# Moving the k^T v and o copies of one attention pair from VectorE and a later place to ScalarE, directly behind a copy out of PSUM

## The chip, the cores and the metric

The kernel runs on one core of a Trainium2 chip. The metric is the device time of one execution in microseconds; lower is better. Within a core several engines run side by side, each through a queue of its own in program order: TensorE (PE in the profile; PEld is its weight load), VectorE (DVE), ScalarE (ACT), GpSimd (POOL) and SyncE (SP), which here issues nearly all DMA transfers. They meet only at semaphores. Matmul results land in PSUM, in banks that have to be read by ScalarE or VectorE before TensorE may write them again.

## The reference

An attention without softmax is normalised and goes through a wide layer with an unusual gate:

```python
kv = einsum('bhsd,bhse->bhde', k, v)          # (8, 8, 64, 64)
o = einsum('bhsd,bhde->bhse', q, kv)          # (8, 8, 576, 64)
x = o / sqrt(mean(o * o, -1) + 1e-6) * g_norm # to (4608, 512)
h = x @ w_in                                  # w_in (512, 2048)
g = h * erf(log(1 + exp(h)))
out = g @ w_out                               # w_out (2048, 512)
```

Inputs q, k, v are fp32 of shape (8, 8, 576, 64); the weights arrive as float64.

## The kernel before, in words

**Groups.** The 4608 tokens are worked on in nine groups of 512: the first 512 tokens of each of the eight batch elements, and a ninth group of the last 64 tokens of all of them, which are collected in `x_last` on the way. Heads are taken in pairs, four pairs to a group. T counts the groups (0 to 8), p the pairs.

**The wide layer.** Groups 0 and 1 go through 16 steps each, n = 0 to 31 (L1188); step f of a group makes 128 of the 2048 hidden columns. In group 1 (T = 1, n = 16 to 31) a step multiplies numbers that were split into a high, a low and a combined part: `hidden` (L855) and `product` (L802) put eight matmuls into the PSUM tile `n_ps` and four into `m_ps`. The two tiles come in turn out of the two banks of `ps_h`, so step n + 1 writes `n_ps` once step n's was read, and `m_ps` likewise. ScalarE copies `n_ps` out, scaled (L1248, "the copy of n"), VectorE adds `m_ps` to it (`add`, L788), ScalarE takes the softplus of the sum (L1262), later the erf (L1186), and VectorE multiplies the two (`gates`, L1114). The last eight hidden tiles of group 1 aren't multiplied with w_out by the plain path: 28 to 31 are taken over by the main loop, and 24 to 27 (`whole - BATCH` to `whole - 1`) are split into `g_held` (`hold_upper` on ScalarE, L748; `hold_lower` on VectorE, L751 and L754) and are multiplied after the loop in `held_sums` (L1142; its matmuls are L1130). `held_sums` first multiplies units 24 and 25 into `o_ps` (they need the combined part, L754) and into two `n_ps`, then unit 26, then unit 27; ScalarE copies the `n_ps` out (`scaled`, L1161). Behind it the main loop over groups 2 to 8 begins (L1355), which fetches the split weights back from DRAM (`load_parts`, L1059, `w_in_parts` and `w_out_parts`); the first four w_out loads can be issued only when the memory of the loop's tiles is free.

**Attention of the next group, inside the steps.** While group 1 goes through its 16 steps, the pairs of group 2, the third group, are prepared: `attention(2, p)` (L454) returns pieces, and `pieces_of` (L1063) lays them into the lists of the steps. `steps[f][3]` and `steps[f][0]` run at the beginning of step f, `steps[f][1]` behind its softplus. For pair p they begin at f = 4p: `visit` (in `steps[4p + 1][1]`) multiplies q with the pair's k^T v, and k with v for the next pair, into a PSUM tile `at_ps` of two banks, and lets ScalarE square o (L492). Then ScalarE copies o out (`copy_out`, L507), the off-diagonal halves of k^T v (`kv_beside`, L368) and the last tokens (L517); `keep` on VectorE adds the halves (`kv_sum`, L372) into `bd_kv`; `sums` on VectorE transposes the squares (L539), sums them in blocks (L415) and brings blocks together (L428, L429). `mean`, `norm` and `split` turn them into the normalised x in three parts.

**The fourth pair of the third group** (T = 2, p = 3, f = 12) is different: `both` is true. From the next group on, pairs are taken two at a time, so it makes k^T v for two pairs. Its `visit` is in step 13 and its `keep` and `sums` at the beginning of step 14 (n = 30). Here the four copies of k^T v halves and the copy of the last tokens are made by VectorE inside `keep`, followed by two sums; and `copy_out` is put into `steps[14][1]`, behind step 14's softplus. Its `mean`, `norm` and `split` are run by `held_sums`.

**Order.** Each engine runs its instructions in the order in which the Python code issues them. So at step 14 VectorE has, one after the other: the gates of step 13, the four copies, `x_last`, the two sums, L539, L415, L428 and L429, step 14's addition (L788), one gate (L1114), and the lower parts of units 24 and 25; at step 15 the addition (L788) and the lower parts of 26 and 27. ScalarE has in step 14: the copy of n, the softplus, the copy of o, the upper parts of units 26 and 27; then step 15's copy of n and softplus, a table load and the roots (L433 to L435), another table load (L1163), and `scaled`.

Of the kernel before, what the change touches and what calls it, by code (L numbers as in the profile page):

```python
# [70 lines left out]
def kernel(  # L71
# [10 lines left out]
    nc = tc.nc  # L82
# [8 lines left out]
    FC = DF // P  # L91
# [242 lines left out]
    def halves_of(t):  # L334
        return t.rearrange("p (a t) -> p a t", a=2)

    def kv_of(T, p):
        return bd_kv[:, (T * NP + p) % 2, :]
# [52 lines left out]
    def other_tile(n):  # L391
        t = attp.tile([P, 2, 2, D], FP32, name="kv_other", tag="kv_other")
        return t[:, 0:n]

    def at_tile():
        return at_pool(1).tile([P, 2, G], FP32, name="at_ps", tag="at")
# [57 lines left out]
    def attention(T, p):  # L454

        st = {}

        alone = p > 1
        then = divmod(T * NP + p + 1, NP)
        both = (T, p) == (FIRST, NP - 1)  # L460
        more_cols = slice(kv_cols.stop, kv_cols.stop + D)

        two = halves_of

        bd = kv_of(T, p)

        def visit():


            qT = ready.pop((T, p))  # L470
            at = st["at"] = at_tile()
            x = halves_of(qT[:, 0:G])
            for s in rows_of:
                nc.tensor.matmul(
                    at[s, 1, 2 * P : 2 * P + R], lhsT=bd[s, D : 2 * D], rhs=qT[s, G:S], start=True, stop=True
                )
            st["o"] = at[:, :, 0 : 2 * P]
            for _, product_ in kv_products(*then, at[:, 1, kv_cols], at[:, 0, kv_cols], first=1):
                product_()
            if both:  # L480
                for _, product_ in kv_products(then[0], 1, at[:, 1, more_cols], at[:, 0, more_cols]):
                    product_()
            for a, i in ((0, 0), (0, 1), (1, 0), (1, 1)):
                nc.tensor.matmul(
                    at[rows_of[i if a else 1 - i], a, 0 : 2 * P],
                    lhsT=bd[rows_of[i], a * D : (a + 1) * D],
                    rhs=x[rows_of[i], a],
                    start=True,
                    stop=True,
                )  # L490
            st["sq"] = qT[:, 0:G]
            nc.scalar.activation(two(st["sq"]), st["o"], AF.Square, scale=0.125)  # L492
            if not both:
                copy_out()
                beside(nc.scalar.copy)

        def copy_out():
            if T < FIRST:
                if T not in xT:
                    xT[T] = wide.tile([P, KC, G], FP32, name="xT", tag="ab"[T])  # L500
                x = xT[T][:, p, :]
            elif p % 2:
                x = x_new.tile([P, G], FP32, name="x", tag="x")
            else:
                x = attp.tile([P, G], FP32, name="x_even", tag="sq_lo")
            st["x"] = x
            nc.scalar.copy(two(x), st["o"])  # L507

        def beside(copy):


            others = st["others"] = other_tile(2)
            at = st["at"]
            kv_beside(at, others[:, 0], copy)
            if both:
                kv_beside(at, others[:, 1], copy, more_cols)
            copy(x_last[:, p, T * R : T * R + R], at[:, 1, 2 * P : 2 * P + R])  # L517

        def keep():
            if both:  # L520
                beside(nc.vector.tensor_copy)
            others = st.pop("others")
            kv_sum(*then, st["at"], others[:, 0])
            if both:
                kv_sum(then[0], 1, st["at"], others[:, 1], more_cols)

        def sums():


            if not alone:  # L530
                if p == 0:
                    shared["ms"] = small_tile("ms")
                total = shared["ms"]
            else:
                total = small_tile("ms")
            st["ms"] = total
            side = p if not alone else 0
            t = attp.tile([P, G], FP32, name="sq_t", tag="rms_r")
            nc.vector.transpose(out=t, in_=st["sq"])  # L539
            sum_blocks(total, side, t)  # L540
            shared[side] = st
            if not alone and p == 0:
                return
            n = side + 1
            other = small_tile("ms_other")
            meet(total, other, nc.vector.tensor_copy, n)
            st["n"] = n

        def root(table=True):
            if "n" not in st:  # L550
                return
            total, n = st["ms"], st["n"]
            st["r"], st["u"] = small_tile("rms"), small_tile("rms_u")
            exp_ln_table()
            roots(total, st["r"], st["u"], n)
            if table:
                softplus_table()

        def norm():
            if "n" not in st:  # L560
                return
            n = st["n"]
            refine(st["ms"], st["r"], st["u"], n)
            for i in range(n):
                other = shared[i]
                rb, x = other.pop("sq"), other["x"]
                spread_over(rb, st["u"], i)
                nc.vector.scalar_tensor_tensor(
                    out=x, in0=x, scalar=gm_col, in1=rb, op0=ALU.mult, op1=ALU.mult
                )  # L570

        def split():
            if T < FIRST or "n" not in st:
                return
            for q_ in range(p + 1 - st["n"], p + 1):
                upper(shared[q_ % 2 if not alone else 0]["x"], x_forms[T][0][:, q_])
            for q_ in range(p + 1 - st["n"], p + 1):
                lower(shared[q_ % 2 if not alone else 0].pop("x"), *(form[:, q_] for form in x_forms[T]))

        def loads():  # L580
            i = T * NP + p + 2
            if i == (FIRST + 1) * NP + 1:
                load_q(i)
                load_kv(i + 1)
                load_kv(i + 2)
                return
            load_pair(i, later=True)
            if i == (FIRST + 1) * NP:
                load_kv(i + 1)

        first_ = (partial(prepare, T, p),) if (T, p) == (1, 0) else ()
        then_ = partial(turn, *then)
        pieces = (first_, (visit, loads), (keep, sums))
        later = copy_out if both else chain
        return (*(partial(chain, *group) for group in pieces), later, root, partial(chain, norm, then_), split)


# [189 lines left out]
    def add(out_, ps):  # L787
        nc.vector.tensor_tensor(out=out_, in0=ps, in1=out_, op=ALU.add)  # L788
# [274 lines left out]
    def pieces_of(T):  # L1063


        steps = [([], [], [], []) for _ in range(FC)]
        for p in range(NP):
            products, apply, after, later, mean, norm, split = attention(T, p)
            f = (BATCH - 1) * (p + 1) if T < FIRST else BATCH * p

            first = T < FIRST and p == 0
            steps[f][1].append(products)
            steps[f + 2 if first else f + 1][3 if first else 1].append(apply)
            steps[f + 3 if first else f + 2][3].append(after)
            steps[f + 2][1].append(later)
            with_erf = (f + 2) % BATCH == BATCH - 1
            if T == FIRST and p == NP - 1:
                ending.extend((partial(mean, table=False), norm, split))
                continue
            steps[f + 2][1].append(partial(mean, table=not with_erf))  # L1080
            steps[f + 3][0].append(norm)
            steps[min(f + 4, FC - 1)][0].append(split)
        return steps
# [104 lines left out]
    for n in range(FIRST * FC + 1):  # L1188
        T, f = divmod(n, FC)
        if T < FIRST:  # L1190
            if f == 0:
                steps = pieces_of(T + 1)
# [47 lines left out]
        if T < FIRST:  # L1240
# [4 lines left out]
            if n in plain:  # L1245
                nc.scalar.copy(h, plain.pop(n))
            else:
                nc.scalar.activation(h, n_ps, AF.Copy, scale=SHIFT - 1.0)  # L1248
                add(h, m_ps)
            if T == FIRST - 1:  # L1250
                if n <= whole + 2:
                    gates(done + max(0, n - whole - 1))
                for key in list(w_new):
                    w_lower(*key)
                for key in to_cut[f]:
                    w_upper(*key)
                if n == whole + 1:
                    gates(whole - 2)
# [225 lines left out]
```

## Time and profile before

| | |
|---|---|
| median of 3 runs | 885.76 us (883.95 to 885.78) |
| profiled execution, its time | 885.19 us |
| its span | 883.4 us |
| PE busy | 873.4 us (99%) |
| DVE busy | 751.2 us (85%) |
| ACT busy | 550.7 us (62%) |
| DMA | 259.88 MB, 293 GB/s to and from HBM over the span |

The span is what the trace covers; the time of the profiled execution is 1.8 us longer. All places in time are us from the span's start, so the steps around the change lie at 209 to 224 us. In a row of the timeline the first number is the start, the second the length; in brackets stands how long the engine had been idle before it, and who released it. A row of the waits has the sum, the times and the longest. "x4" is a row of four instructions merged into one.

### The profile page before, as it was taken

To read this page: it belongs to the slowest core of one execution; us is meant where nothing else is said; L and a number is where in the kernel's file an instruction comes from. 1 tells how busy PE (TensorE), PEld (TensorE's weight loads), DVE (VectorE), ACT (ScalarE), POOL (GpSimd) and SP (SyncE) were. 2 spreads that over 40 slices of the span, in tenths; PEclk is the share of its full clock that TensorE was granted. 3 is DMA by queue.
4 is the path that set the end of the run, shared out by engine and by line. 5 is a ranking of instruction groups with operands and counts; after the bars stand their busy time and mean duration, and the time that the engine had idled before them with its cause. 6 is when DMAs were issued, how large, how long until landed. Compare 5 with 4: busy or idle time off the path is not lost.

```text
span 883.4 us, 13264 instructions
## 1 busy us (share of the span) xinstructions
PE 873.4 (99%) x4842; PEld 653.1 (74%) x4842; DVE 751.2 (85%) x1122; ACT 550.7 (62%) x808; POOL 4.7 (1%) x14
## 2 busy tenths in 40 slices
PE   8999999999999999999999999999999999999998
PEld 4444455565778888888888888888888888888887
DVE  5889987899889898989898989898979797966667
ACT  5967675686675657565665647474757575755552
POOL 2000000000000000000000000000000000000000
PEclk9999999999999999999999999999999999999999
DMA  9976428889699987998799979998887779778861
GB/s 288 292 253 183 147 75 326 311 314 355 229 341 411 341 346 246 395 326 347 232 379 350 351 236 349 374 328 297 281 344 281 293 267 359 294 275 334 314 257 48
DMA packets 136928, 259.88 MB, mean 294 GB/s; under 512 B 78816, under 2 KB 87264, under 8 KB 136864
## 3 DMA queue, kind: packets, MB, share of 16 engines
q1 hardware_dynamic: 136128, 258.09, 82.2%
q10 hardware_dynamic: 544, 0.82, 0.3%
q8 instruction: 38, 0.62, 0.3%
q14 instruction: 26, 0.21, 0.1%
q0 software_dynamic: 192, 0.13, 0.1%
HBM read 224.40 MB, written 34.60 MB: 293 GB/s over the span
## 4 chain that ended last, share of the span: by engine, by line
PE 81%; DVE 9%; ACT 4%; DMA 3%; issue 2%; SPq 0%; DVEq 0%; ACTq 0%
PE n_ps L813 47%; PE m_ps L813 24%; PE h_ps L1233 3%; PE o_ps L869 2%; DVE w_e L287 1%; DMA w_out_parts<-w_out 1%; PE diag_ps L636 1%; PE at_ps L641 1%; DVE h_sb L1114 1%; DVE w_e L284 1%; DVE w_new L775 1%; PE o_ps L1130 1%; PE warm_ps L1017 1%; DVE w_e L281 1%; DMA w_raw<-in_moe_w_out_dram 1%
## 5 line engine op out<-in xcount | busy, mean ns | idle before, releaser
L813 PE MATMUL n_ps<-w_out_parts,g_forms 128*128 128x512 f32 (+1 forms) x936 | 229.9, 388 | 0.8 <-DMA w_out_parts<-w_out 0.8
L813 PE MATMUL n_ps<-x_forms,w_in_parts 128*128 128x512 f32 x896 | 222.6, 390 | 0.0
L813 PEld LDWEIGHTS n_ps<-w_out_parts,g_forms 128*128 128x128 f32 x936 | 175.1, 188 | 37.1 <-DMA w_out_parts<-w_out 1.2
L813 PEld LDWEIGHTS n_ps<-x_forms,w_in_parts 128*128 128x128 f32 x896 | 167.4, 188 | 38.3 <-issue 3.9
L788 DVE TENSOR_TENSOR h<-m_ps,h 128x512 f32<-128x512 f32 x116 | 78.5, 686 | 65.6 <-PE m_ps L813 65.5
L1395 ACT ACTIVATE s<-h 128x512 f32<-128x512 f32 x112 | 69.2, 632 | 88.1 <-DVE h L788 88.1
L813 PE MATMUL m_ps<-w_out_parts,g_forms 128*128 128x512 f32 x464 | 123.9, 389 | 0.0
L1390 ACT ACTIVATE h<-n_ps 128x512 f32<-128x512 f32 x112 | 66.7, 597 | 85.5 <-PE n_ps L813 83.2
L813 PE MATMUL m_ps<-x_forms,w_in_parts 128*128 128x512 f32 x448 | 119.7, 389 | 0.0
L813 PEld LDWEIGHTS m_ps<-w_out_parts,g_forms 128*128 128x128 f32 x464 | 87.1, 188 | 18.1
L813 PEld LDWEIGHTS m_ps<-x_forms,w_in_parts 128*128 128x128 f32 x448 | 84.1, 188 | 17.5
L788 DVE TENSOR_TENSOR e<-m_ps,e 128x512 f32<-128x512 f32 x116 | 80.2, 692 | 14.0 <-PE m_ps L813 3.7
L869 PE MATMUL o_ps<-w_out_sb,h_sb 128*128 128x512 f32 x192 | 87.1, 596 | 0.1
L748 ACT ACTIVATE g_forms<-h 128x1024 fp32r<-128x1024 f32 x58 | 60.8, 1060 | 39.5 <-PE m_ps L813 21.2
L754 DVE SCALAR_TENSOR_TENSOR g_forms<-g_forms 128x1024 fp32r<-128x1024 f32 x58 | 71.1, 1225 | 2.0
L751 DVE TENSOR_TENSOR g_forms<-h,g_forms 128x1024 fp32r<-128x1024 f32 x58 | 70.5, 1216 | 0.5 <-ACT g_forms L748 0.4
L869 PEld LDWEIGHTS o_ps<-w_out_sb,h_sb 128*128 128x128 f32 x192 | 35.9, 190 | 42.4 <-issue 37.7
L1444 DVE TENSOR_TENSOR h<-h,s 128x1024 f32<-128x1024 f32 x56 | 65.9, 1217 | 0.0
L783 DVE SCALAR_TENSOR_TENSOR e<-n_ps,e 128x512 f32<-128x512 f32 (+1 forms) x89 | 59.8, 672 | 3.7 <-PE n_ps L813 3.7
L1233 PE MATMUL h_ps<-xT,w_in_sb 128*128 128x512 f32 x128 | 57.8, 595 | 0.7 <-DVE w_in_sb L292 0.7
L117 ACT ACT_TABLE_LOAD x41 | 52.6, 1283 | 0.7
L1418 ACT ACTIVATE s<-s 128x1024 f32<-128x1024 f32 x50 | 50.6, 1054 | 0.3
(160 smaller groups left out, 918.5 us busy)
## 6 DMA issues: line engine op xcount, KB each, us to landing
w_out_parts<-w_out SPq DMA_DIRECT2D x116, 768.0 KB, 7.5
w_in_parts<-w_in SPq DMA_DIRECT2D x112, 768.0 KB, 7.0
w_in<-w_new SPq DMA_DIRECT2D x16, 768.0 KB, 5.0
k_sb<-in_k_dram SPq DMA_DIRECT2D x32, 288.0 KB, 6.0
v_sb<-in_v_dram SPq DMA_DIRECT2D x31, 288.0 KB, 6.0
w_raw<-in_moe_w_in_dram SPq DMA_DIRECT2D x16, 512.0 KB, 5.6
w_raw<-in_moe_w_out_dram SPq DMA_DIRECT2D x8, 1024.0 KB, 5.0
out_dram<-e SPq DMA_DIRECT2D x32, 256.0 KB, 4.0
```

Source lines behind the costliest of these rows:

```text
L117: nc.scalar.preload_act_table_set("softplus")
L748: nc.scalar.activation(high, x, AF.Copy, scale=1.0 + 2.0**-13)
L751: nc.vector.tensor_tensor(out=low, in0=x, in1=high.bitcast(FP32), op=ALU.subtract)
L754: nc.vector.scalar_tensor_tensor(out=both, in0=low.bitcast(FP32), scalar=SHIFT, in1=high.bitcast(FP32), op0=ALU.mult, op1=ALU.add,)
L783: nc.vector.scalar_tensor_tensor(out=out_, in0=ps, scalar=scale, in1=out_, op0=ALU.mult, op1=ALU.add)
L788: nc.vector.tensor_tensor(out=out_, in0=ps, in1=out_, op=ALU.add)
L813: nc.tensor.matmul(ps[:, cols], lhsT=weights(form, k), rhs=moving(form, k)[:, cols], start=(form == forms[0] and k == 0), stop=(form == fo ...
L869: nc.tensor.matmul(o_ps[j], lhsT=g[:, j * P : j * P + P], rhs=one(w_out_sb, f), start=(f == 0), stop=last,)
L1233: nc.tensor.matmul(plain[i], lhsT=blocks_of(one(w_in_sb, i % FC))[:, c], rhs=xT[T][:, c, :], start=(c == 0), stop=(c == KC - 1),)
L1390: nc.scalar.activation(h[:, i], n_ps, AF.Copy, scale=SHIFT - 1.0)
L1395: nc.scalar.activation(s[:, i], h[:, i], AF.Softplus)
L1444: nc.vector.tensor_tensor(out=part(h, half), in0=part(h, half), in1=part(s, half), op=ALU.mult)
```

## The change

In pair (2, 3) alone the five copies out of `at_ps` go from VectorE to ScalarE, and with the copy of o they are put into a fifth list of the step, which is run directly behind step 14's copy of n and its addition, ahead of the softplus. The two sums (`keep`) go to the beginning of step 15. `sums` stays at the beginning of step 14. All other pairs issue what they issued before.

```diff
             st["sq"] = qT[:, 0:G]
             nc.scalar.activation(two(st["sq"]), st["o"], AF.Square, scale=0.125)
             if not both:
-                copy_out()
-                beside(nc.scalar.copy)
+                copies()
+
+        def copies():
+            copy_out()
+            beside(nc.scalar.copy)
...
         def keep():
-            if both:
-                beside(nc.vector.tensor_copy)
             others = st.pop("others")
             kv_sum(*then, st["at"], others[:, 0])
             if both:
...
-        pieces = (first_, (visit, loads), (keep, sums))
-        later = copy_out if both else chain
+        pieces = (first_, (visit, loads), (sums,) if both else (keep, sums))
+        later = (copies, keep) if both else ()
...
-        steps = [([], [], [], []) for _ in range(FC)]
+        steps = [([], [], [], [], []) for _ in range(FC)]
...
             steps[f + 3 if first else f + 2][3].append(after)
-            steps[f + 2][1].append(later)
+            if later:
+                steps[f + 2][4].append(later[0])
+                steps[f + 3][3].append(later[1])
...
                 nc.scalar.activation(h, n_ps, AF.Copy, scale=SHIFT - 1.0)
                 add(h, m_ps)
+            for piece in steps[f][4]:
+                piece()
             if T == FIRST - 1:
```

## The prediction, made before the changed kernel was run

> **What bounds the kernel now.** I read the head of the page first, then the chain that ended last around the change, then the timeline there, the waits, and last the engines' busy time with the granted clock in stretches of 3.4 us.
>
> ```profile
> span 883.4 us, 13264 instructions
> ...
> PE 873.4 (99%) x4842; PEld 653.1 (74%) x4842; DVE 751.2 (85%) x1122; ACT 550.7 (62%) x808; POOL 4.7 (1%) x14
> ```
>
> TensorE is busy for 99% of the span, so only work ahead of one of its few pauses can be worth anything. The change lies at 213 to 222 us, and there the chain leaves TensorE (rows of the chain: start, length, what):
>
> ```profile
> 214.84 0.29 DVE kv_other L368
> ...
> 216.31 0.39 DVE bd_kv L372 x2
> ...
> 218.91 0.68 DVE h L788
> ...
> 221.58 3.62 PE o_ps L1130 x8
> ...
> 230.28 0.60 ACT e L1161
> ...
> 236.97 0.69 DVE h L1114
> ...
> 240.47 9.80 DMA w_out_parts<-w_out
> ...
> 250.32 0.72 PE n_ps L813 x2
> ...
> 254.71 1.81 PE n_ps L813 x8
> ```
>
> The reader is to see that the chain runs through VectorE without a break from 214.84 to 221.5, through exactly the copies (L368) and sums (L372) that the change touches; that TensorE takes it over at 221.58; and that it goes on through ScalarE's copy at 230.28, VectorE, and the load of a w_out part to 250.32, from where it is TensorE, at 1.81 / 8 = 0.227 us a matmul. The timeline gives the times (start, length):
>
> ```profile
> 213.55 1.28 DVE L1114 TENSOR_TENSOR h_sb<-h_sb,s_sb 128x512 f32<-128x512 f32 x2
> ...
> 214.20 0.58 ACT L492 ACTIVATE qT<-at_ps 128x512 f32<-128x512 f32 x1
> ...
> 214.84 1.21 DVE L368 COPY kv_other<-at_ps 64x128 f32<-64x128 f32 x4
> ...
> 215.72 0.58 ACT L1248 ACTIVATE h<-n_ps 128x512 f32<-128x512 f32 x1
> 216.09 0.23 DVE L517 COPY x_last<-at_ps 128x64 f32<-128x64 f32 x1
> ...
> 216.62 0.70 DVE L539 STREAM_TRANSPOSE sq_t<-qT 128x512 f32<-128x512 f32 x1
> ...
> 218.08 0.39 PE L813 MATMUL n_ps<-x_low,w_new 128*128 128x512 f32 x1
> ...
> 219.63 0.63 ACT L1262 ACTIVATE s_sb<-h 128x512 f32<-128x512 f32 x1 [3.33 <-DVE h L788]
> ...
> 219.65 1.20 PE L813 MATMUL m_ps<-x_both,w_new 128*128 128x512 f32 x4 [1.19 <-DVE h L788]
> ...
> 220.17 0.57 ACT L507 COPY x<-at_ps 128x512 f32<-128x512 f32 x1
> 220.64 1.15 ACT L748 ACTIVATE g_held<-h_sb 128x512 fp32r<-128x512 f32 x2
> 220.83 0.69 DVE L754 SCALAR_TENSOR_TENSOR g_held<-g_held 128x512 fp32r<-128x512 f32 x1
> ...
> 221.58 3.62 PE L1130 MATMUL o_ps<-w_place,g_held 128*128 128x512 f32 x8 [0.72 <-DVE g_held L754]
> ...
> 221.69 0.59 ACT L1248 ACTIVATE h<-n_ps 128x512 f32<-128x512 f32 x1
> 222.16 0.69 DVE L754 SCALAR_TENSOR_TENSOR g_held<-g_held 128x512 fp32r<-128x512 f32 x1
> 222.77 0.68 DVE L788 TENSOR_TENSOR h<-m_ps,h 128x512 f32<-128x512 f32 x1
> ...
> 224.08 0.69 DVE L754 SCALAR_TENSOR_TENSOR g_held<-g_held 128x512 fp32r<-128x512 f32 x1
> ...
> 225.41 0.69 DVE L754 SCALAR_TENSOR_TENSOR g_held<-g_held 128x512 fp32r<-128x512 f32 x1
> ...
> 226.24 1.28 ACT L1163 ACT_TABLE_LOAD   x1
> ```
>
> TensorE pauses twice. Step 15's m_ps lies in the bank that step 14's addition (L788 at 218.91) must have read; that addition stands behind the k^T v work in VectorE's queue, and TensorE waits 1.19 us for it. Then the held products (L1130) wait 0.72 us for the first g_held (L754 at 220.83). ScalarE, for its part, stands idle 3.33 us before the softplus at 219.63. The stretches show what the pauses bring with them (columns: stretch, its length, busy us and instructions of PE, PEld, DVE, ACT, POOL, then the granted clock, DMA share, GB/s):
>
> ```profile
> 218.40:221.80 3.40, 1.49 (x6) 0.90 (x6) 3.31 (x9) 2.17 (x5) 0.00 (x0) 1.00 0.99 410
> 221.80:225.20 3.40, 3.40 (x9) 2.57 (x9) 3.33 (x6) 2.18 (x3) 0.00 (x0) 0.50 1.09 324
> ...
> 248.00:251.40 3.40, 2.63 (x12) 1.84 (x11) 3.33 (x5) 1.75 (x6) 0.00 (x0) 1.00 1.06 331
> ```
>
> After the stretch in which TensorE worked only 1.49 of 3.40 us it runs one whole stretch at half clock, and so loses 3.40 x 0.50 = 1.7 us more. A stretch with 2.63 us of work, at 248, was not followed by a drop in the rows.
>
> **The change, part by part.** *Removed from VectorE at step 14:* four copies, the copy to x_last and both sums, all ahead of the transpose L539. That starts at 216.62; afterwards it can start where the copies did, 214.84, since the square it reads (L492) ends at 214.20 + 0.58 = 214.78. That is 1.78 us off every VectorE instruction down to the second g_held. The transpose's wait on ScalarE is new; it was covered by the copies, and if the square were later, each us would come off the gain. By these rows it costs 0 to 0.1 (a semaphore's way, estimated from 221.52, the end of L754, to 221.58, the start of L1130). The addition then ends at 219.59 - 1.78 = 217.81, the first two g_held at 219.74 and 221.07.
>
> *Added to ScalarE at step 14, ahead of the softplus:* four copies and x_last, with o's copy moved forward. What they cost on ScalarE has rows from the other pairs (min, median, max ns):
>
> ```profile
> L368 ACT COPY kv_other<-at_ps x14: 257/260/263, 46.5 to 189.2; 64x128 f32<-64x128 f32 x14
> L517 ACT COPY x_last<-at_ps x7: 212/213/213, 47.1 to 189.5; 128x64 f32<-128x64 f32 x7
> ```
>
> 0.57 + 4 x 0.26 + 0.21 = 1.82 us behind the copy of n that ends at 216.30: to 218.12. The softplus was waiting until 219.63, so this lies inside the 3.33 us; it would now be ready at 217.81, starts at 218.12 and ends at 218.75. Queued behind it are two g_held copies (1.15) and step 15's copy of n (0.59), which ends at 220.5 in place of 222.28. Cost on the path: nothing; without that cover it would be 1.82.
>
> *Moved on VectorE:* the two sums (0.39 in the chain) now stand between the second g_held and step 15's addition. Their new wait on ScalarE (218.12) is over 2.9 us before VectorE comes to them. Behind them stand the addition, which frees the bank of TensorE's second held n_ps, and the third and fourth g_held. These come 1.78 - 0.39 = 1.39 us earlier: addition done at 222.06, g_held at 223.38 and 224.71. The bd_kv they write is first read at 240.26:
>
> ```profile
> 240.26 0.27 PE L636 MATMUL diag_ps<-qT,bd_kv 64*64 64x64 f32 x2
> ```
>
> No DMA is added or moved, and the order on TensorE, SyncE and GpSimd is the same in both kernels.
>
> *TensorE then.* The last n_ps matmul of step 15 starts at 218.08, matmuls follow each other by 0.227, and the bank is free at 217.81: m_ps starts at 218.31 without a wait and ends at 218.31 + 3 x 0.227 + 0.39 = 219.4. The first g_held is there at 219.74, so L1130 starts at 219.79 (before 221.58). Four matmuls at full clock take 0.91, to 220.70; the second four wait for 221.07 and run 221.12 to 222.03. Idle time in all: 0.4 + 0.4 us, where it was 1.91. With 3.40 - 0.8 = 2.6 us of work this is next to the row at 248 (2.63, no drop) and far from the one at 218.4 (1.49), so I take the clock as held. Then 8 + 8 + 6 matmuls with no wait (third and fourth g_held are early): 222.03 + 22 x 0.227 = 227.03. ScalarE's copy L1161, which took over at 230.28, then starts at 227.05; its table load at 226.24, 3.5 us behind the addition's start, ends at 221.38 + 4.75 = 226.13 and isn't later. **Sum: 230.28 - 227.05 = 3.2 us.** At full clock the kernel before would have run four matmuls from 221.58, waited for the second g_held (222.16 + 0.69) and come to 222.90 + 26 x 0.227 = 228.8: so 1.7 of the 3.2 is the shorter VectorE chain and 1.5 the clock.
>
> The Trainium skill bears on this (TensorE: Matmul & The Clock Gate, "What's actually happening" and "HAM oscillation — how this bites in real kernels"): it puts the clock's watch in free-running windows of about 3.4 us and warns of idle gaps longer than that. The length of the drop here, 3.40 us, agrees; the gap rule doesn't, since the longest gap before the drop is 1.19 us. By the gap rule the drop at 221.8 doesn't come from these waits and would stay, which is the first rival below.
>
> *Does it last to the end?* Behind L1161 the path is VectorE (L1114 at 236.97), the loads of w_out, and a wait of 0.8 us for the fourth part.
>
> ```profile
> SPq L1059 <- DVE h L1114: 8.5, 1, 8.5
> ...
> PE n_ps L813 <- DMA w_out_parts<-w_out: 0.8, 1, 0.8
> ...
> 233.00:234.00 1.00, 1.00 (x6) 0.82 (x5) 1.00 (x3) 0.92 (x2) 0.00 (x0) 1.00 0.02 7
> ```
>
> The load's issue waits for VectorE and nothing else (8.5 us), and the DMA engines are empty from 233 on (share 0.02 in that row). Issued 3.2 us earlier, at about 234.5, it still meets empty engines. So TensorE's need and the transfer move together and the 0.8 stays. If the transfer gained more than TensorE, 0.8 more could come off: lower bound 881.2. From 250 on the chain is TensorE.
>
> The profiled execution took 885.19 us: 885.19 - 3.2 = 882.0. The median of the runs shown is 0.57 higher (885.76), which would give 882.6. I forecast 882.2. The lowest run shown, 883.95, is 1.8 below the median, about the price of one clock drop; that it had none can't be seen.
>
> **The rivals.** *The half clock stays* (at 221.8, or at a window that catches both remaining pauses). For it: one drop only is in the trace, so its threshold is known just to lie between 1.49 and 2.63 us of work in 3.40, and my 2.6 is near the upper end. Against: it is on the good side by every row. TensorE then loses 1.7 us between 221.8 and 225.2; the held n_ps ends at 228.73 and the gain is 1.5: 883.7, from the median 884.3.
>
> *The gain ends at the w_out load.* Were the fourth part to land at 250.27 as before, TensorE would only wait longer: 885.2, no change. For it: the path goes through a transfer of 9.80 us. Against: its issue hangs on VectorE alone and the engines are idle before.
>
> *ScalarE becomes the bound: slower.* The place is the block of six copies at 216.30. It decides from 3.33 us on, where the softplus comes later than before; every us above goes through step 15's copy of n and its addition to g_held and TensorE. With copies 2.8 times as slow (1.82 to 5.1 us) the end comes 1.8 us later: 887.0, and with the half clock repeated later up to 888.7. For it: six ScalarE reads of one PSUM tile in a row while TensorE writes other banks. Against: 14 and 7 such copies in the trace differ by 6 ns and 1 ns, in steps that had the same neighbours.
>
> **How the numbers follow.** Forecast 0.70; half clock stays 0.15; gain lost at the load 0.08; ScalarE the bound 0.07. The range holds the first two and reaches to the lower bound: 881.0 to 884.6; left out are the last two with 0.15 and a little at the edges. About 0.2% (1.8 us) is what a measurement of this kernel can tell from no change. Faster by more: 0.67 of the first case's 0.70 and 0.05 of the second, 0.72. Within it: 0.03 + 0.10 + 0.08 = 0.21. Slower: 0.07.
>
> **What would show it.** Right: no wait of m_ps on L788, a granted clock of 1.00 from 218 to 226, L1130 begun about 1.8 us earlier and L1161 about 3.2, the copies on ScalarE at 0.26 with the softplus directly behind them, the wait for the fourth w_out part still about 0.8. Wrong: a half-clock stretch near 222, a longer wait at w_out_parts, or an n copy of step 15 that ends after 222.3.

## The result, and the profile after

The changed kernel took 882.32 us (median of 22 runs, 880.72 to 885.05). The kernel before, timed beside it, took 884.44 us (22 runs, 882.36 to 885.82). The ratio is 0.9977, with a 95% interval of 0.9969 to 0.9985: faster by 0.23%, clear of noise. The forecast was 882.2 us.

The profiled execution took 882.89 us. The page's head shows it:

```profile
span 881.1 us, 13264 instructions
...
PE 871.8 (99%) x4842; PEld 652.6 (74%) x4842; DVE 750.1 (85%) x1117; ACT 551.5 (63%) x813; POOL 4.7 (1%) x14
```

The span is 2.3 us shorter than before. Five VectorE instructions have gone to ScalarE. The line numbers are up by 1 to 5: L540 was L539, L789 was L788, L755 was L754, L1133 was L1130, L1164 was L1161, L1251 was L1248, L1267 was L1262. The timeline around the change (start, length):

```profile
213.77 1.28 DVE L1117 TENSOR_TENSOR h_sb<-h_sb,s_sb 128x512 f32<-128x512 f32 x2
...
214.42 0.58 ACT L492 ACTIVATE qT<-at_ps 128x512 f32<-128x512 f32 x1
...
215.03 0.71 DVE L540 STREAM_TRANSPOSE sq_t<-qT 128x512 f32<-128x512 f32 x1
...
216.07 0.60 ACT L1251 ACTIVATE h<-n_ps 128x512 f32<-128x512 f32 x1
...
217.16 1.07 ACT L368 COPY kv_other<-at_ps 64x128 f32<-64x128 f32 x4
...
217.33 0.69 DVE L789 TENSOR_TENSOR h<-m_ps,h 128x512 f32<-128x512 f32 x1
...
218.25 0.21 ACT L520 COPY x_last<-at_ps 128x64 f32<-128x64 f32 x1
218.35 0.64 ACT L1267 ACTIVATE s_sb<-h 128x512 f32<-128x512 f32 x1
...
218.66 1.09 PE L814 MATMUL m_ps<-x_both,w_new 128*128 128x512 f32 x4
...
219.93 0.59 ACT L1251 ACTIVATE h<-n_ps 128x512 f32<-128x512 f32 x1
220.00 0.77 PEld L1133 LDWEIGHTS o_ps<-w_place,g_held 128*128 128x128 f32 x4 [0.69 <-DVE g_held L755]
220.00 2.52 PE L1133 MATMUL o_ps<-w_place,g_held 128*128 128x512 f32 x8 [0.25 <-DVE g_held L755]
...
221.19 0.48 DVE L372 TENSOR_TENSOR bd_kv<-at_ps,kv_other 128x128 f32<-128x128 f32 x2
221.59 0.68 DVE L789 TENSOR_TENSOR h<-m_ps,h 128x512 f32<-128x512 f32 x1
...
227.55 0.60 ACT L1164 ACTIVATE e<-n_ps 128x512 f32<-128x512 f32 x1 [1.21 <-PE n_ps L1133]
```

The gates that stand ahead of the change start 0.22 us later in this execution than in the one of before (213.77 against 213.55), so 0.22 is to be taken off in a comparison. The reader is to see that VectorE goes from the gates straight into the transpose (215.03, no copies between), that step 14's addition comes at 217.33 (before 218.91), that m_ps of step 15 has no wait in brackets any more, and that L1133 starts at 220.00 (before 221.58), 1.80 us earlier on the common scale. On ScalarE the copies run at 1.07 / 4 = 0.27 us each, and the softplus stands directly behind them without a wait.

The busy times and the granted clock in stretches of 3.4 us (columns as in the prediction), and the waits of TensorE in this part:

```profile
218.40:221.80 3.40, 3.04 (x12) 1.86 (x11) 3.33 (x8) 2.11 (x5) 0.00 (x0) 1.00 1.01 403
221.80:225.20 3.40, 3.40 (x17) 2.79 (x16) 3.18 (x6) 2.80 (x6) 0.00 (x0) 1.00 1.10 326
```

```profile
PE n_ps L814 <- DMA w_out_parts<-w_out: 1.2, 1, 1.2
...
PE o_ps L1133 <- DVE g_held L755: 0.2, 1, 0.2
PE n_ps L1133 <- ACT e L1164: 0.2, 1, 0.2
```

TensorE works 3.04 of 3.40 us where it worked 1.49, and the clock stays at 1.00. The wait for the fourth w_out part is 1.2 us here and was 0.8. The chain has the load as in before:

```profile
237.51 10.47 DMA w_out_parts<-w_out
...
248.02 0.73 PE n_ps L814 x2
```

L1164, ScalarE's copy, starts 2.95 us earlier on the common scale, and the matmul behind the load 2.52 us earlier (248.02 against 250.32 + 0.22); the rest went into the longer wait.

### The profile page after: what moved, and what is told of

The parts are those of the page before. It is cut to its first block, busy times and chain, and to the rows that moved or that the text cites. A ratio compares the mean times of both kernels' runs of the same rounds, so it can differ in the third digit from the quotient of the medians.

```text
span 881.1 us, 13264 instructions
## 1 busy us (share of the span) xinstructions
PE 871.8 (99%) x4842; PEld 652.6 (74%) x4842; DVE 750.1 (85%) x1117; ACT 551.5 (63%) x813; POOL 4.7 (1%) x14
## 4 chain that ended last, share of the span: by engine, by line
PE 80%; DMA 7%; DVE 5%; ACT 4%; SPq 2%; issue 1%; DVEq 0%; ACTq 0%
PE n_ps L814 48%; PE m_ps L814 24%; PE h_ps L1236 3%; PE o_ps L870 3%; DVE w_e L287 1%; DMA w_out_parts<-w_out 1%; DMA w_raw<-in_moe_w_in_dram 1%; PE diag_ps L637 1%; DMA w_in_parts<-w_in 1%; PE at_ps L642 1%; DMA q_sb<-in_q_dram 1%; DMA v_sb<-in_v_dram 1%; SPq L184 1%; DVE w_e L284 1%; DMA w_in<-w_new 1%
## 5 line engine op out<-in xcount | busy, mean ns | idle before, releaser
L789 DVE TENSOR_TENSOR h<-m_ps,h 128x512 f32<-128x512 f32 x116 | 78.5, 686 | 64.9 <-PE m_ps L814 64.8
L789 DVE TENSOR_TENSOR e<-m_ps,e 128x512 f32<-128x512 f32 x116 | 80.2, 692 | 14.4 <-PE m_ps L814 3.2
L755 DVE SCALAR_TENSOR_TENSOR g_forms<-g_forms 128x1024 fp32r<-128x1024 f32 x58 | 71.1, 1226 | 2.0
```

The costliest lines, as they stand in the source:

```text
L755: nc.vector.scalar_tensor_tensor(out=both, in0=low.bitcast(FP32), scalar=SHIFT, in1=high.bitcast(FP32), op0=ALU.mult, op1=ALU.add,)
```

## The experiments

Two theories stood against each other, with two side questions. **A**: the price was VectorE's time ahead of step 14's addition, and the pauses that it made bring the half clock. **B**: the half clock has nothing to do with these pauses. **C**: what counts is ScalarE, the place of the copies or VectorE being rid of them anywhere. **D**: the load of w_out ends when it does, whatever its issue. Line numbers in the rows are those of each run's own kernel; the tiles' names tell which instruction it is.

The kernel before was timed beside them again. In 100 of its runs for which the mean clock is listed, the median is 884.26 us; 40 runs have a mean clock of 0.998 or less, with a median of 885.18, and 60 have more, with 883.67. One stretch of 3.4 us at half clock is 1.7 of 883 us, 0.2%, so 0.998 is what one such drop leaves; where in the run it lies the mean doesn't say, only a trace does. The changed kernel has one such run in 31 (885.05), of which there is no trace; the other 30 have a median of 882.30.

**e1: work in the pause.** Edit on the kernel before; the needless matmuls run in step 15 alone.

```diff
-            n_ps, m_ps = hidden(T, f, turns=False)
+            n_ps, m_ps = hidden(T, f, turns=False, again=5 if f == FC - 1 else 0)
...
+        for _ in range(again):
+            nc.tensor.matmul(n_ps, lhsT=weights(0, 0), rhs=moving(0, 0), start=True, stop=True)
         for ps, forms, cols in runs:
```

> The kernel before, with five needless matmuls into n_ps at the head of step 15's product, written over by the product itself; they fall into the 1.19 us in which TensorE waits for m_ps's bank. Theory A (the half clock at 222 comes from the two pauses): the pause before m_ps is under 0.3 us, granted clock 1.00 from 218 to 226, L1130's eight o_ps matmuls start at about 221.6 as before but take about 2.3 us in place of 3.6, and the time is about 1.5 us below a profile of before that has the drop: about 883.7 in every run, with mean clock 1.000 in every run. Against the median of before (884.44, runs with and without a drop) about -0.7. Rival B (the drop has nothing to do with these pauses): the drop stays in the trace and the time is equal or up to 1.1 us longer.

Measured: 883.56 us (11 runs), ratio 0.9993 (0.9978 to 1.0007). All 11 runs have a mean clock of 0.999 or 1.000. From the timeline on TensorE, and the stretch:

```profile
216.31 1.43 PE L811 MATMUL n_ps<-x_high,w_new 128*128 128x512 f32 x5
...
219.61 1.19 PE L815 MATMUL m_ps<-x_both,w_new 128*128 128x512 f32 x4
```

```profile
218.40:221.80 3.40, 2.62 (x11) 1.56 (x10) 3.32 (x8) 2.21 (x5) 0.00 (x0) 1.00 1.01 416
```

m_ps starts at 219.61 as before, now with no pause listed ahead of it, and no stretch at half clock follows. With no drop in 11 runs, where before has 40 in 100, B falls. The median is that of before's runs without a drop (883.67): the five matmuls cost nothing that can be measured, and the clock is all that this edit repairs.

**e10: the same work elsewhere**, in step 12 (`again=5 if f == FC - 4`).

> The kernel before with the five needless matmuls of the run e1_fill_pause, but at the head of step 12's product, where TensorE doesn't wait. Theory A: they cost their 5 x 0.227 = 1.1 us, or less where a later wait takes some of it up (the pauses at 219 to 221 hang on VectorE, which isn't moved by the same amount): between 884.4 and 885.5, drops as often as in before; not below it as in e1_fill_pause. Rival (any additional TensorE work in this region helps the clock): below before.

Measured: 884.35 us (11 runs), ratio 1.0004 (0.9995 to 1.0012). One run has a drop (886.47); the ten others have a median of 884.31, 0.6 above before's runs without one, so here the matmuls cost about half of their 1.1 us. In its trace TensorE's wait for m_ps fell from 1.2 us to 0.6, since VectorE had not moved:

```profile
PE m_ps L815 <- DVE h L788: 0.6, 1, 0.6
```

That also shortened the pause, and the drops were fewer than expected. That drops would be as frequent as before was wrong, and it speaks for the pause as their cause.

**e2: the copies stay on VectorE, at step 15.**

```diff
-        pieces = (first_, (visit, loads), (keep, sums))
-        later = copy_out if both else chain
+        pieces = (first_, (visit, loads), (sums,) if both else (keep, sums))
+        later = (copy_out, keep) if both else ()
...
-            steps[f + 2][1].append(later)
+            if later:
+                steps[f + 2][1].append(later[0])
+                steps[f + 3][3].append(later[1])
```

> The kernel before, with only the place changed: the five copies and the two sums stay together on VectorE, but at the beginning of step 15; o's copy stays behind the softplus. Theory A (what counts is VectorE's queue ahead of step 14's addition and of each g_held): the addition and the first two g_held come 1.8 us earlier than before, no wait of m_ps, no half clock; step 15's addition and the third and fourth g_held as late as before, so TensorE waits about 0.5 us more in front of them than the changed kernel does; the last held n_ps of j = 0 about 0.9 us later than in the changed kernel: about 883.2. Rival C (what counts is that VectorE is rid of the copies, wherever they stand): about as before, 884.4 to 885.2.

Measured: 883.05 us (12 runs). The ratio is 0.9994 (0.9982 to 1.0005), unclear, because two runs lie at 886.2 and 886.6; both have a mean clock of 0.998. The profiled one of them shows that this drop isn't the one at 222:

```profile
246.60:250.00 3.40, 0.93 (x5) 0.46 (x4) 3.03 (x4) 2.72 (x6) 0.00 (x0) 1.00 1.04 323
250.00:253.40 3.40, 3.40 (x10) 2.67 (x9) 1.38 (x2) 3.36 (x5) 0.00 (x0) 0.53 0.91 300
```

Here TensorE waited 2.5 us for the fourth w_out part, and the half clock followed that. The ten runs without a drop have a median of 882.80, half a us above the changed kernel. Ahead of that drop the trace gives a second measure, the way from the gates of step 13 to ScalarE's first copy of a held n_ps:

```profile
213.00 1.28 DVE L1116 TENSOR_TENSOR h_sb<-h_sb,s_sb 128x512 f32<-128x512 f32 x2
...
227.91 0.60 ACT L1163 ACTIVATE e<-n_ps 128x512 f32<-128x512 f32 x1 [0.83 <-PE n_ps L1132]
```

That is 14.91 us, against 13.78 in the changed kernel (213.77 to 227.55) and 15.59 in e11 below, which has the instructions of before up to there and no drop. So a part of the chain's gain comes from the place in VectorE's queue alone, 0.7 of 1.8 us by this measure and 0.9 of 1.4 by the medians, and the rest from VectorE being rid of the copies; which share is the larger stays open.

**e3: ScalarE's copies behind the softplus** (`steps[f + 2][1].append(later[0])` in the changed kernel).

> The changed kernel with ScalarE's six copies behind step 14's softplus, where o's copy was, in place of ahead of it. Theory A: step 15's copy of n ends about 1.7 us later than in the changed kernel, at about 222.2, step 15's addition and the last two g_held about 0.7 us later, but TensorE comes to them late enough: 0 to 0.3 us over the changed kernel, 882.3 to 882.6. Rival C (the place directly behind the copy of n carries the gain): 0.7 us or more, 883.0 and up.

Measured: 882.17 us (11 runs), ratio 0.9975 (0.9964 to 0.9986), as the changed kernel. The place directly behind the copy of n is worth nothing that can be measured.

**e4: the sums directly behind the copies** (`steps[f + 2][4].append(later[1])` in the changed kernel).

> The changed kernel with the two sums directly behind ScalarE's copies in step 14, not at the beginning of step 15. Theory A: VectorE waits for ScalarE's last copy (about 0.4 us) and then does 0.4 us of sums ahead of the gate, so the first two g_held come about 0.9 us later and the last two about 0.5; TensorE's pause before L1133 grows from 0.25 to about 1.2 us, and its work in the 3.4 us around it falls to about 1.8: the end is 0.8 us later (883.1) where the clock holds, 2.3 (884.6) where it drops; this is between the two loads with a known answer (1.5 drops, 2.6 holds). Rival C: the sums' place is of no account, 882.3.

Measured: 883.10 us (11 runs), no drop in any, ratio 0.9988 (0.9979 to 0.9997). The rows:

```profile
218.49 0.49 DVE L372 TENSOR_TENSOR bd_kv<-at_ps,kv_other 128x128 f32<-128x128 f32 x2 [0.33 <-ACT x_last L520]
...
220.96 2.53 PE L1133 MATMUL o_ps<-w_place,g_held 128*128 128x512 f32 x8 [1.23 <-DVE g_held L755]
```

```profile
218.40:221.80 3.40, 2.17 (x10) 1.43 (x8) 3.24 (x7) 2.23 (x5) 0.00 (x0) 1.00 1.02 417
```

VectorE waits 0.33 us for ScalarE and L1133 pauses 1.23: the step later is worth 0.8 us. A single pause of 1.23 us didn't bring the half clock.

**e6: both engines copy.** The changed kernel, with VectorE's five copies added again ahead of the transpose, into a tile that nothing reads.

```diff
         def sums():
+            if both:
+                spare = attp.tile([P, G], FP32, name="spare", tag="rms_r")
+                two_ = spare[:, 0 : 2 * P].rearrange("p (n a e) -> p n a e", n=2, a=2)
+                for n, cols in enumerate((kv_cols, more_cols)):
+                    kv_beside(st["at"], two_[:, n], nc.vector.tensor_copy, cols)
+                nc.vector.tensor_copy(out=spare[:, 2 * P : 2 * P + R], in_=st["at"][:, 1, 2 * P : 2 * P + R])
```

> The changed kernel, and VectorE makes the five copies too, into a spare tile that nothing reads, ahead of the transpose as in the kernel before. Theory A (the gain is VectorE's time ahead of the addition, and the clock): the transpose starts about 1.4 us later than in the changed kernel, m_ps waits about 0.8 us for the addition, L1133 starts about 1.4 us later, the clock may drop again: 883.7 without a drop, 885 with one. Rival C (what counts is what ScalarE does and when): as the changed kernel, 882.3.

Measured: 884.26 us (12 runs), ratio 1.0001 (0.9992 to 1.0011). Three runs have a drop. The waits in its trace:

```profile
PE m_ps L820 <- DVE h L795: 0.9, 1, 0.9
...
PE o_ps L1139 <- DVE g_held L761: 0.7, 1, 0.7
```

With ScalarE as in the changed kernel and VectorE as before the pauses are back, and with them the time and the drops. So what ScalarE does carries none of the gain by itself; with e3 for the place, and e2 for being rid of the copies anywhere, C falls.

**e5 and e8: the last gates first.** The changed kernel with the end of `held_sums` in another order.

```diff
-        erf((whole + 2,))
-        scaled(3)
-        erf((whole + 3,))
+        erf((whole + 2, whole + 3))
+        scaled(3)
+        for n in (whole + 2, whole + 3):
+            gates(n)
...
-    for n in range(whole + 2, FIRST * FC):
-        gates(n)
```

> The changed kernel; after the loop the last two erfs go ahead of the fourth copy of n_ps on ScalarE and the last two gates ahead of the last two additions to e on VectorE. Theory A (part of the gain was given back at the w_out load, whose issue waits for the last gate and whose fourth part lands 10 us behind it): the four w_out loads are issued about 1.2 us earlier than in the changed kernel, TensorE's wait for the fourth part falls from 1.2 us to 0 to 0.3, the time by about 0.9 to 1.2: about 881.3. Rival D (the load ends when the DMA engines are through with other traffic, not by its issue): wait and time as in the changed kernel, 882.3.

> The run e5_gates_first once more, the same text, for its spread beside the changed kernel on one chip. Theory A: median about 881.3, all runs within about 1 us, none with a mean clock of 0.998 or less. Rival (its five runs were lucky ones): a spread of 3 us and more as in the changed kernel, median 881.8 or more.

> The changed kernel once more, as the neighbour of the run e8_gates_first_again. Theory A: median about 882.3, spread from 881 to 883.5 and now and then 885.

Measured: e5 881.27 us (5 runs, 881.03 to 881.75; ratio 0.9965, 0.9953 to 0.9977) and e8 881.09 us (5 runs, 880.10 to 882.56; ratio 0.9965, 0.9952 to 0.9979), none with a drop; the changed kernel beside e8 882.31 us (e9, 9 runs, 880.90 to 883.02; ratio 0.9974, 0.9964 to 0.9984). In e5's trace the loads go out 1.26 us earlier than in the changed kernel (there at 234.98), and TensorE goes through the fourth part without a break:

```profile
233.72 3.21 SPq L1060 DMA_DIRECT2D w_out_parts<-w_out  x4
```

```profile
245.22 1.98 PE L814 MATMUL n_ps<-w_out_parts,g_forms 128*128 128x512 f32 x8
247.04 1.07 PE L814 MATMUL m_ps<-w_out_parts,g_forms 128*128 128x512 f32 x4
```

This version beats both kernels, by 1.1 us the changed one. Two details were missed: e8's spread is 2.5 us, not 1, and its profiled execution still waits 0.7 us for w_out, where e9's, the changed kernel's second profile, doesn't wait at all. The wait differs from execution to execution by more than the issue moves, so one pair of traces can't refute D. The medians do, and the profiles taken together fit them: six of the nine with the old order wait for the fourth part, 0.5 to 2.5 us, and one of the five with the gates first, 0.7 us.

**e7 and e11: the same order in the kernel before.**

> The kernel before, with only the reordering of the last two erfs and gates of the run e5_gates_first. Theory A (the wait for the fourth w_out part is a second, separate loss, behind the change's place; the half clock at 222 is another): no wait on w_out_parts in the trace, runs with a mean clock of 0.998 or less still there in about two of five; median about 0.8 to 1.0 us below before, 883.4 to 883.6, runs without a drop about 882.6, with one about 884.3. Rival D (the load's end doesn't hang on its issue): as before, 884.3.

> The run e7_before_gates_first once more, since its 12 runs had the half clock 9 times where before has it in 32 of 79. Theory A (a drop more often was chance; taken by clock it was 0.7 us below before in both kinds): drops in about two of five runs, runs without a drop about 882.7, with one about 884.4, median about 883.4. Rival (the reordering itself makes drops more frequent, so nothing is won): drops in two of three or more, median 884.2.

Measured: e7 884.29 us (12 runs; ratio 1.0002, 0.9993 to 1.0011), e11 883.28 us (11 runs; ratio 0.9988, 0.9979 to 0.9997). e7's median was a miss: neither profile waits for w_out any more, but nine of e7's 12 runs had the half clock, against three of 11 in e11. Both together by clock: 12 runs with a drop 884.44, 11 without 882.90, against 885.18 and 883.67 in before, so 0.7 to 0.8 us less in each kind. The w_out wait and the drop at 222 are two losses that add. Whether the reordering changes how often the drop comes is not shown: its edit lies behind the place of the drop, and 12 in 23 against 40 in 100 isn't clear of chance.

The two profiles answer another question, why the drop comes in some runs only. Both executions have the same two pauses (1.2 and 0.7 us); e7's has the drop and e11's hasn't. In each of the 14 traces the records of the granted clock change only at places that lie whole multiples of 3.413 us apart, and these places differ from execution to execution. Cut there, e7's stretches are

```profile
218.53:221.94 3.41, 1.57 (x6) 1.00 (x7) 3.33 (x8) 2.31 (x5) 0.00 (x0) 1.00 0.99 398
221.94:225.35 3.41, 3.41 (x10) 2.56 (x9) 3.34 (x6) 2.19 (x3) 0.00 (x0) 0.50 1.11 352
```

and e11's

```profile
217.07:220.48 3.41, 2.22 (x10) 1.32 (x8) 3.27 (x10) 1.05 (x3) 0.00 (x0) 1.00 1.01 407
220.48:223.89 3.41, 2.57 (x10) 1.68 (x10) 3.31 (x7) 2.19 (x5) 0.00 (x0) 1.00 1.12 360
223.89:227.30 3.41, 3.41 (x17) 2.81 (x16) 3.12 (x7) 3.31 (x6) 0.00 (x0) 1.00 0.86 229
```

In e7 one stretch holds both pauses; in e11 a border lies between them. From the first rise of the clock on, every such stretch of the 14 traces with at most 1.57 us of TensorE's work is followed by half clock, and every one with 1.94 us or more by the full one; none lies between. The 1.94 is e6's:

```profile
218.75:222.16 3.41, 1.94 (x7) 1.34 (x8) 3.34 (x7) 2.16 (x4) 0.00 (x0) 1.00 1.02 420
222.16:225.57 3.41, 3.28 (x14) 2.37 (x14) 3.38 (x7) 1.85 (x2) 0.00 (x0) 1.00 1.07 332
```

e11's trace also shows the price of the drop, since up to ScalarE's first copy of a held n_ps it runs before's instructions:

```profile
213.35 1.28 DVE L1114 TENSOR_TENSOR h_sb<-h_sb,s_sb 128x512 f32<-128x512 f32 x2
...
228.94 0.60 ACT L1161 ACTIVATE e<-n_ps 128x512 f32<-128x512 f32 x1 [1.61 <-PE n_ps L1130]
```

From the gates to this copy it takes 15.59 us; with the drop it is 16.73 in before (213.55 to 230.28) and 16.77 in e7.

**e12: both repairs of e1 and e5 in the kernel before**, VectorE's queue at step 14 untouched.

> The kernel before with both repairs that leave VectorE's queue at step 14 as it is: the five needless matmuls of e1_fill_pause and the reordering of e5_gates_first. Neither the half clock nor the w_out wait should be left, so what remains between it and e5_gates_first (881.2) is VectorE's chain alone. Theory A: no run with a mean clock of 0.998 or less, median 882.5 to 882.9, so 1.3 to 1.7 us above e5_gates_first. Rival C (the chain is of no account, the clock and the w_out wait are all): 881.2.

Measured: 883.12 us (11 runs, 882.59 to 883.56; ratio 0.9981, 0.9972 to 0.9990), no drop, no wait for w_out in its trace. What is left against e5 and e8 together (881.20) is 1.9 us, a little over what was expected: VectorE's chain alone. From the gates of step 13 to the first copy of a held n_ps it takes 15.59 us in e12's trace and 13.81 in e5's, 1.8 us.

## Why the prediction was right

**VectorE's queue ahead of the addition** was the term that carries the forecast, at 1.78 us for L1130's start; it measured 1.80. At ScalarE's first copy of a held n_ps the chain alone was to bring 1.7 us, and the traces without a drop give 15.59 - 13.78 = 1.81. e6 shows that it is this queue and not ScalarE, e2 that the place alone does a part of it.

**ScalarE's block** was costed at nothing because of the 3.33 us of idle time. From the end of n's copy (216.07 + 0.60) to the softplus at 218.35 it took 1.68 us where 1.82 was worked out, and e3 shows that even the place behind it costs nothing.

**The sums a step later**: 1.39 us of gain at step 15's addition were forecast. It came at 221.59 where it had been at 222.77, so 1.18 + 0.22 = 1.40. e4 prices the step at 0.8 us.

**The clock** was right in kind, and mis-sized in price and in how often. The forecast put 1.5 us of its 3.2 on the drop. At the same copy the traces show 1.14 (before) and 1.18 (e7) against e11. The working had both of its ends about 0.3 us too early: for before at full clock it gave 228.8, where e11 has 228.94 + 0.20 = 229.14 on the common scale, and for the changed kernel 227.05, where 227.55 - 0.22 = 227.33 was measured. Their difference, the chain, came out right, but the measured 230.28 less 228.8 made the clock too large. By the medians, runs with a drop are 885.18 - 883.67 = 1.5 us longer than runs without; where the 0.3 us beyond the trace lie isn't shown. And the drop comes in 40 of 100 runs: 0.6 us on average. The Trainium skill (TensorE: Matmul & The Clock Gate, "HAM oscillation — how this bites in real kernels") warns of gaps above about 3.4 us. The traces don't agree: in before and e7 pauses of 1.2 and 0.7 us within one stretch of 3.413 sufficed, and e1 shows that they are the cause. What the Trainium skill says of windows that run freely (same page, "What's actually happening") is borne out by the traces: the borders lie 3.413 us apart, and at other places in e11 (217.07) than in e7 (218.53).

**The w_out load** was to move with everything else and its wait to stay at 0.8. It didn't stay: 1.2 in the changed kernel's first profile, none in its second, 2.5 in e2. That step took a wait that varies for one that is fixed. Issuing the loads earlier brings 1.1 us by e5 and e8 against the changed kernel, and 0.7 to 0.8 by e7 and e11 against before.

**The sum.** Chain alone: 1.7 forecast; measured in time 883.67 - 882.30 = 1.4 between runs without a drop, 882.90 - 881.20 = 1.7 and 883.12 - 881.20 = 1.9 where the w_out wait is taken out too. Clock: 0.6 on average in place of 1.5. Together 2.0 to 2.1 of the 884.26 of before, which gives 882.2 to 882.3. The forecast came to that place from 885.19, the time of an execution with a drop, less 3.2, which is 882.0; between this and the 882.6 from the median it took 882.2 without a reason. So the mechanism was right, but that the number fell within 0.2 us is in part luck: the two profiled executions differ by 2.3 us, not 3.2, because the clock brought 0.3 less, the longer wait at w_out took 0.4 and the later start of the second 0.2. The difference to the median of before, 2.1 us, was smaller than the sum too, and only 0.3 above the 1.8 that the forecast called the bound of what can be told from no change.

Of the rivals, the half clock that stays at 222 is not in the two profiles of the changed kernel. One of its 31 runs has a drop; where isn't known, and e2's shows that one can also follow the wait for w_out. The gain lost at the load is not seen, though 0.4 us of it went there in the first profile. ScalarE as the bound is refuted by the rows above: 0.27 us a copy, and step 15's copy of n, at 219.93, ends well ahead of 222.3.

## What to carry to other kernels

A copy that is nobody's bottleneck can still cost its full length, as here 1.8 us, if it stands in an engine's queue ahead of the read that frees a PSUM bank: look at what stands between the release that TensorE waits for and the engine's last free moment. A short pause of TensorE can cost twice, once itself and once through the clock, if it falls into one stretch of the clock together with others. Where the stretches begin changes from run to run, so a sum against one profiled execution has to say whether that execution had the drop and how many runs do. When a loss is repaired upstream, look at the next transfer whose issue hangs on the same chain: here moving two gates ahead of two additions was worth another 1.1 us.

## What the runs showed of the hardware

In the 14 traces the granted clock changes only at borders 3.413 us apart, which lie at other places in each execution. A stretch between two borders with at most 1.57 us of TensorE's work was followed by one at half clock, one with 1.94 us or more never was. So pauses of 1.2 and 0.7 us brought the drop in e7, where one stretch held both, and none in e11, where a border parted them; 40 of 100 runs of before have a mean clock of 0.998 or less. A single pause of 1.23 us (e4) brought none in 11 runs, and one of 2.5 us (e2) brought one. Five matmuls whose results are thrown away, placed in the pause, cost no time that could be measured, and all 11 runs kept a mean clock of 0.999 or 1.000. The landing of the same four w_out loads varied between executions of one program: the wait behind them was 1.2 and 0 us in two profiles of the changed kernel, 0 and 0.7 in two of the version with the gates first.
